# One block of linear attention and gated FFN on one core: accumulators of the last tiles moved into PSUM ahead of their passes, k weights counted by halves, and a new order of all work

## The chip, the cores and the metric

The kernel runs on one core of a Trainium2 chip. The metric is the device time of one execution in microseconds. A core has five engines that run on their own and wait for each other by semaphores: TensorE (PE, with its weight loads as PEld), VectorE (DVE), ScalarE (ACT), GpSimd (POOL) and SyncE (SP), which issues all DMAs here.

## What is computed

A residual block over 2048 tokens of width 512, everything in float32:

```python
xn = layernorm(x)                               # (2048, 512)
# A: linear attention, 32 heads of 16
q, k, v = split(xn @ wqkv)
pq, pk = phi(q), phi(k)                         # phi(t) = (t+1 if t>0 else exp(t)) + 1e-6
kv, z = pk^T v, sum(pk)                         # per head
s = ((pq @ kv) / (pq @ z + 1e-6)) @ wo
# B: gated FFN, inner width 1792
g = silu((gelu(xn @ w_gate) * (xn @ w_up)) @ w_down)
out = x + s * g
```

## The kernel before

**Precision and products.** Each float32 operand is split into a high part (a cast to fp32r on ACT, `split`'s `copy`) and a low part (source minus high part, on DVE or POOL, `split`'s `tt`). A product is three passes: high by high, and the two mixed ones (`three`). Products of 2 by 2 blocks are formed with seven instead of eight block products (`PRODUCTS`): sums of the products are built up in PSUM banks X, Y, Z (attention) and FX, FY, FZ (FFN). Bank X or FX takes several products one after the other; between two of them ACT copies the sum so far out (`saved`, `esaved`: tiles e1, u2, u3, fe1, fu2, fu3), and the next product is added onto the bank.

**Stages.** First x is loaded tile by tile (128 tokens), normalised (`ln`: statistics st, mv, ve on DVE, rstd on POOL, xn on DVE), transposed on TensorE into PSUM (pt) and split (Xh, Xl). The first four tiles, two pairs, take k and q by plain products: 12 matmuls a tile for k (`plain`, tiles k00 to k11), then 12 for q. Their weights are the k columns of `wqkv`, loaded in four requests of 256 KB: the two halves of wk1 and of wk2, which `kq_split` splits into kq. Then the other pairs go by block products, and gps gathers pk^T xn. After that the FFN of one half of the tokens runs (`ffn(1, ...)`), with the rest of the attention in between (pkv, pm, sps), and at the end the FFN of the other half (`ffn(0, finish0)`). An FFN goes over 28 quarter weights q (`quad`), with down products into accumulators `acc` by groups of units (`down`, groups [0], [1, 2], [3, 4], [5, 6]); the first group copies its bank into acc on ACT, the later ones add theirs on DVE. Behind the last group `finish0` takes silu of acc, multiplies it by s (fs, read back from DRAM), adds x (fx) and stores. The last tile (j = 7) is done in two column halves (`halves`).

**Order.** No engine's order is written out by hand. Every operation is recorded in `Plan` with an engine, a cost, its predecessors and a due time (`late`); `forward` lays them out one after the other, on each engine that one first that is ready and due earliest, and TensorE may take an operation up to `AHEAD` = 6 us out of the stated turn. It keeps one shared port for POOL and those DVE operations that don't touch PSUM, and it gives DMAs a landing time from `RATES`. Then `altered` changes due times at random, from a seed: it picks a place where TensorE waits within a stretch of turns, and shifts due times around it. The seeds that are applied are listed in `KEPT`, by stretch. So whatever changes a cost, a dependency or a seed can move any instruction on any engine. How the planner scores a seed is this:

```python
for lo, hi, draws in KEPT:
    for n in draws:
        best = self.altered(n, lo, hi, pe, *best)
```

The dependencies that matter for the change: `kq_split` used `raw[:, i]`, a view that stands for both halves of the weight, so a half was planned as if it needed both loads. In `down`, the last group ended with

```python
do("DVE", dve(D // m), lambda o, i: nc.vector.tensor_add(o, o, i), a, ps, name="acc")
```

and `finish0` then called `silu`, which works on acc in place.

Of the kernel before, what the change touches and what calls it, by code (L numbers as in the profile page):

```python
# [16 lines left out]
EPS_LN = 1e-5  # L17
EPS = 1e-6
KEPT = [
    (-1, 12, [3200031, 3200084, 3200113, 3200368]),  # L20
    (605, 9999, [3200013, 3200102, 3200161, 3200247]),
]

TABLES = {"exp": "exp", "gelu": "gelu", "silu": "silu"}
LOAD = 1.28

RATES = 215.0, 380.0

HELD = 1.9

# [55 lines left out]
class Plan:  # L86
# [71 lines left out]
    def altered(self, n, lo, hi, pe, _, done, late):  # L158
        draw = random.Random(n)
        for o in self.ops:  # L160
            o.late = late[o]
        waits = [w for w in self.waits(done) if lo <= w[0] < hi]
        if not waits:
            return _, done, late
        w = draw.choices(waits, [w[1] for w in waits])[0]
        if draw.random() < 0.5:
            for o in self.chain(done, w[2]):
                if draw.random() < 0.7:
                    o.late -= draw.uniform(0.0, 4.0)
        else:  # L170
            at, back = w[2].late, draw.uniform(1.0, 12.0)
            share, far = draw.choice((0.05, 0.2, 0.5)), draw.uniform(0.2, 4.0)
            for o in self.ops:
                if at - back < o.late < at + 2.0 and draw.random() < share:
                    o.late += draw.uniform(-far, far)
        new = self.forward(pe)
        return max(t for t, _ in new), new, {o: o.late for o in self.ops}
# [83 lines left out]
    def forward(self, pe):  # L261
        for o in self.ops:
            o.left, o.ready, o.end, o.lat, o.behind = len(o.pre), 0.0, None, o.lat0, []
        cands = {e: [] for e in self.HOP}
        free = dict.fromkeys(self.HOP, 0.0)
        port = dma = 0.0
        for o in self.ops:
            if not o.left:
                cands[o.eng].append(o)
        done, first, table, last = [], 0, "exp", {}  # L270
        while any(cands.values()):
            best = None
            while first < len(pe) and pe[first].end is not None:
                first += 1
            for e, c in cands.items():
                if e == "PE":
                    c = [o for o in c if o.turn <= pe[first].turn + self.AHEAD]
                if not c:
                    continue
                ready = {}  # L280
                for o in c:
                    t = o.ready
                    for g in o.banks:
                        p = last.get(g)
# [12 lines left out]
                if best is None or (t, asked) < best[:2]:  # L297
                    best = t, asked, o
            t, asked, o = best
            cands[o.eng].remove(o)  # L300
            if o.table and o.table != table:
                t, table = t + LOAD, o.table

            took = o.cost - (min(self.CUT[o.eng], t - asked) if o.port else 0.0)

            if o.eng == "PE" and t > free["PE"] + 0.02:
                took += 0.1
            free[o.eng] = o.end = t + took
            for g in o.banks:
                if g in last and last[g].eng != o.eng:  # L310
                    o.behind.append(last[g])
                last[g] = o
            if o.port:
                port = o.end
            if o.eng == "SP":

                dma = max(dma, o.end) + o.kb * (1.4 if o.kb == 896 else 1.0) / (RATES[0] if o.end < 3.0 else RATES[1])
                o.lat = max(dma - o.end, o.kb / self.RATE) + (0.9 if o.end < 8.0 else HELD)
            done.append((o.end, o))
            for q in o.suc:  # L320
                q.ready = max(q.ready, o.end + self.gap(o, q))
                q.left -= 1
                if not q.left:
                    cands[q.eng].append(q)
        assert len(done) == len(self.ops)
        return done
# [15 lines left out]
def kernel(  # L342
# [96 lines left out]
    def split(hi, lo, src, n, name="", eng="DVE"):  # L439
        copy("ACT", hi, src, n, name + "h")  # L440
        tt(eng, "sub", lo, src, hi, n, name + "l")
# [85 lines left out]
    def kq_split(slot, raw, k, n=1, eng="DVE"):  # L527
        r = 4 * ORDER.index(slot)
        if n == 2 and r // 7 == (r + 3) // 7:
            h = KQ[r // 7].part(KQR[slot, 0], (slice(None), slice(r % 7, r % 7 + 2)))  # L530
            lo = KQ[r // 7].part(KQR[slot, 1], (slice(None), slice(r % 7 + 2, r % 7 + 4)))
            split(h, lo, raw, n * D, f"kq{slot}", eng)
        else:
            for i in range(k, k + n):
                split(kq(slot, 0, i), kq(slot, 1, i), raw[:, i], D, f"kq{slot}", eng)

    tokens = [(8 * (n // 4) + n % 4, 8 * (n // 4) + 4 + n % 4) for n in range(NP)]

# [227 lines left out]
    for n in range(NP):  # L766
        if n == 0:
            ln(tokens[n][1])
        else:
            ln(*tokens[n])  # L770
        for i in range(2):
            load_next()
            transp(n, i)
            split_x(n, i)
            if n < CL:
                if i:
                    b = tile_in("up", 19 + n, [P, 2, 2, P], F32R, f"b12_{n}", 2)
                    b12[n] = [b.part(b.res[lo:lo + 1], (slice(None), lo)) for lo in range(2)]
                    split(*b12[n], pts[n, 1][:, 0:2], 2 * P, "b12")
                if 2 * n + i == 3:  # L780
                    gacc(first_g)
                split_xn(tokens[n][i])
                k_out(plain(n, i, False), tokens[n][i])
        if n >= CL:
            forms(n)
            if n < 2 * CL:
                forms(n - CL)
                spill_x(n - CL)
            if n < 4:
                spill_x(n)  # L790
            rest(n, first_products(n))
            for t in tokens[n]:
                gacc(t)
        if n == CL - 1:
            for t in seq[1:2 * CL]:
                gacc(t)
            for m in range(CL):
                for i in range(2):
                    q_out(plain(m, i, True), tokens[m][i])
# [162 lines left out]
    def down(p, units_, is_first, is_last, finish):  # L962
        for j in range(8):
            key = (11, 21) if j < 4 else (12, 22)
            sl = slice((j % 4) * P, (j % 4 + 1) * P)
            m = halves(p, units_, j)
            if is_first:
                acc[p, j] = tile_in("up", FACC[j], [P, D], F32, f"acc{p}_{j}", 2 if halves(p, groups[-1], j) > 1 else 1)
            for c in range(m):
                ps = bank(ring("down", [5, 6, 7]), f"d{p}_{units_[0]}_{j}{c}", (P, D // m))  # L970
                cs = slice(c * D // m, (c + 1) * D // m)
                total = Sum(ps)
                for u in units_:
                    hh, hl = hs[p, u, key[0]], hs[p, u, key[1]]
                    dh, dl = dws[p, u]
                    total.add(("D", p, u, j, c), *three([(h[0][:, sl], h[1][:, sl]) for h in (hh, hl)],
                                                       [(dh[:, i, cs], dl[:, i, cs]) for i in range(2)]),
                              name="down", cost=PASS if m == 1 else SHORT)
                a = columns(acc[p, j], c, m)
                if is_first:  # L980
                    copy("ACT", a, ps, D, "acc")
                else:
                    do("DVE", dve(D // m), lambda o, i: nc.vector.tensor_add(o, o, i), a, ps, name="acc")  # L983
            if is_last:
                finish(p, j)

    groups = [[0], [1, 2], [3, 4], [5, 6]]

    def silu(p, j, n=1):
        for i in range(n):  # L990
# [164 lines left out]
    def finish0(p, j):  # L1155
# [3 lines left out]
        dma(sr, s_d(j, slice(j * P, (j + 1) * P)), 256)  # L1159
        dma(xr, ext(x[j * P:(j + 1) * P, :]), 256)  # L1160
        w = D // n
        silu(p, j, n)
        for i in range(n):
            so = columns(sr, i, n)
            do("DVE", dve(w), lambda o, a: nc.vector.tensor_mul(o, o, a), so, columns(acc[p, j], i, n))
# [36 lines left out]
```

## Time and profile before

| | us |
|---|---|
| median of 3 runs | 625.42 (625.35 to 626.65) |
| the profiled execution | 625.18 |
| its span | 623.2 |
| PE busy | 615.2 (99%) |
| DVE, ACT, POOL busy | 408.5, 319.1, 233.0 |
| granted clock of TensorE | 0.997 |

The profile is of one execution; times in it count from the start of its span. In the chain of work that ended last, each line is a start, a duration and what ran. In the timeline, a line is a start, a duration, the engine, the line of the kernel, the operation with output and inputs, and in brackets how long the engine had been idle and what ended that. In the waits, the columns are the total, the number of times and the longest.

### The profile page before, as it was taken

The page shows a single profiled execution, that of the slowest core. Times are in us where ns is not written, and L with a number is a line of the kernel's source. Part 1 is how long each engine was busy: PE and PEld are TensorE (multiplying, and loading weights), DVE is VectorE, ACT ScalarE, POOL GpSimd, SP SyncE. Part 2 cuts the span into 40 slices and gives each one's busy share as a digit, 9 for nine tenths or more (in the row PEclk, how much of TensorE's full clock was granted, in tenths as well). Part 3 has the DMA queues.
Part 4 walks back from the last instruction along what each step waited for, and adds up shares of the span by engine and source line. Part 5 has one row for each costly group of instructions (what it writes and reads, how often), then busy time and mean ns, then how long its engine had stood idle before and what let it go on. Part 6 is the DMA issues. An engine that isn't in the chain of part 4 may idle for free.

```text
span 623.2 us, 7828 instructions
## 1 busy us (share of the span) xinstructions
PE 615.2 (99%) x2782; PEld 506.1 (81%) x2782; DVE 408.5 (66%) x648; ACT 319.1 (51%) x571; POOL 233.0 (37%) x239
## 2 busy tenths in 40 slices
PE   8999999999999999999999999999999999999996
PEld 6887888888888888888888788888888888888885
DVE  6999998787626643762448799657366427732466
ACT  6777777887556523650345332276656316612431
POOL 4447754366624520460046334044334404300110
PEclk9999999999999999999999999999999999999998
DMA  7249822135221211220169566841221212001163
GB/s 246 74 150 311 262 73 69 68 103 167 68 67 35 64 39 35 67 68 0 44 186 387 181 210 209 306 134 37 65 60 43 68 34 68 1 1 34 35 198 140
DMA packets 52440, 68.68 MB, mean 110 GB/s; under 512 B 2864, under 2 KB 31792, under 8 KB 52400
## 3 DMA queue, kind: packets, MB, share of 16 engines
q1 hardware_dynamic: 52400, 68.17, 34.0%
q8 instruction: 22, 0.36, 0.3%
q14 instruction: 18, 0.15, 0.1%
HBM read 49.28 MB, written 18.87 MB: 109 GB/s over the span
## 4 chain that ended last, share of the span: by engine, by line
PE 98%; DVE 0%; DMA 0%; ACT 0%; issue 0%; POOL 0%; DVEq 0%
PE FX L460 25%; PE d L460 24%; PE FZ L460 12%; PE sps L460 7%; PE gps L460 7%; PE FY L460 6%; PE X L460 5%; PE Z L460 3%; PE k L460 2%; PE q L460 2%; PE Y L460 1%; PE pt L624 1%; PE ptq L1115 1%; PE pkv L1075 1%; PE pm L1087 1%; DMA x<-in_A_x 0%
## 5 line engine op out<-in xcount | busy, mean ns | idle before, releaser
L460 PE MATMUL FX<-Xh,w 128*128 128x512 f32 x448 | 134.4, 391 | 0.0
L937 POOL TENSOR_TENSOR h<-h,g 128x512 f32<-128x512 f32 x42 | 59.5, 1416 | 179.1 <-DVE h L437 179.1
L460 PEld LDWEIGHTS FX<-Xh,w 128*128 128x128 f32 x448 | 83.5, 188 | 18.8 <-ACT fu L431 1.7
L437 POOL TENSOR_TENSOR tmp<-raw 128x256 f32<-128x256 f32 x56 | 45.0, 822 | 93.0 <-DVE w L437 77.9
L460 PE MATMUL d<-dwh,hh 128*128 128x512 f32 (+1 forms) x228 | 69.7, 388 | 0.0
L460 PE MATMUL d<-dwh,hl 128*128 128x512 f32 (+1 forms) x228 | 69.2, 385 | 0.0
L460 PE MATMUL FX<-Xl,w 128*128 128x512 f32 x224 | 69.1, 390 | 0.0
L460 PE MATMUL FZ<-Xh,w 128*128 128x512 f32 x224 | 69.0, 389 | 0.0
L460 PE MATMUL d<-dwl,hh 128*128 128x512 f32 (+1 forms) x228 | 68.9, 385 | 0.0
L983 DVE TENSOR_TENSOR acc<-acc,d 128x512 f32<-128x512 f32 (+1 forms) x49 | 33.0, 673 | 48.6 <-PE d L460 48.5
L431 ACT CAST hh<-h 128x512 fp32r<-128x512 f32 x56 | 34.6, 620 | 56.6 <-PE d L460 27.9
L431 ACT COPY fu<-FX 128x512 f32<-128x512 f32 x56 | 32.7, 584 | 42.3 <-PE FX L460 42.2
L460 PEld LDWEIGHTS d<-dwl,hh 128*128 128x128 f32 x228 | 42.6, 188 | 8.7
L460 PEld LDWEIGHTS d<-dwh,hl 128*128 128x128 f32 x228 | 42.5, 188 | 8.6
L460 PEld LDWEIGHTS d<-dwh,hh 128*128 128x128 f32 x228 | 42.3, 188 | 8.8 <-issue 0.5
L460 PEld LDWEIGHTS FX<-Xl,w 128*128 128x128 f32 x224 | 42.0, 188 | 8.9
L460 PEld LDWEIGHTS FZ<-Xh,w 128*128 128x128 f32 x224 | 42.1, 188 | 8.7
L437 DVE TENSOR_TENSOR w<-raw,w 128x512 fp32r<-128x512 f32 (+1 forms) x56 | 44.9, 807 | 1.7 <-ACT w L431 1.6
L437 DVE TENSOR_TENSOR hl<-h,hh 128x512 fp32r<-128x512 f32 x56 | 39.0, 700 | 9.6 <-ACT hh L431 9.6
L437 DVE TENSOR_TENSOR w<-tmp,w 128x512 fp32r<-128x512 f32 x56 | 38.4, 693 | 6.8 <-ACT w L431 6.5
L431 ACT CAST dwh<-draw 128x1024 fp32r<-128x1024 f32 x14 | 14.7, 1049 | 47.3 <-PE d L460 45.1
L437 DVE TENSOR_TENSOR g<-fu,FZ 128x512 f32<-128x512 f32 x28 | 19.1, 683 | 30.0 <-PE FZ L460 27.0
(160 smaller groups left out, 1206.5 us busy)
## 6 DMA issues: line engine op xcount, KB each, us to landing
raw<-in_B_w_gate SPq DMA_DIRECT2D x14, 512.0 KB, 3.8
raw<-in_B_w_up SPq DMA_DIRECT2D x14, 512.0 KB, 3.8
draw<-in_B_w_down SPq DMA_DIRECT2D x14, 512.0 KB, 3.4
x<-in_A_x SPq DMA_DIRECT2D x16, 256.0 KB, 4.3
q_d<-qp SPq DMA_DIRECT2D x16, 256.0 KB, 2.0
q<-q_d SPq DMA_DIRECT2D x16, 256.0 KB, 3.6
xh_d<-Xh SPq DMA_DIRECT2D x4, 896.0 KB, 5.5
xl_d<-Xl SPq DMA_DIRECT2D x4, 896.0 KB, 7.3
```

The source lines that it names most:

```text
L431: do("ACT", act(n), lambda o, i: nc.scalar.copy(o, i), dst, src, name=name)
L437: do(eng, c, lambda o, p, q: getattr(e, f"tensor_{op}")(o, p, q), dst, a, b, name=name)
L460: nc.tensor.matmul(o, a, b, start=not self.on and self.made == 1, stop=self.made == self.passes, skip_group_check=self.on)
L624: nc.tensor.transpose(o[:, k, :], a[:, k * P:(k + 1) * P], b)
L937: do("POOL", pool(NC), lambda o, i: nc.gpsimd.tensor_mul(o, o, i), h, g, name="h")
L983: do("DVE", dve(D // m), lambda o, i: nc.vector.tensor_add(o, o, i), a, ps, name="acc")
L1075: nc.tensor.matmul(o[:, g, :], a[:, c, g * P:(g + 1) * P], b[:, c, g * P:(g + 1) * P], start=(c == 0), stop=(c == KT - 1))
L1087: do("PE", 0.9, lambda o, a, b, g=g: nc.tensor.matmul(o, a[:, g, :], b[:, g, :], start=True, stop=True), pm, kv4, wo_sb, key=("m", g))
L1115: nc.tensor.transpose(o[:, k, :], a[:, k * P:(k + 1) * P], b)
```

## The change

Five things are changed. In `down`, for the tiles from `LATE` = 6 on of the last group of the last FFN half, ACT copies the accumulator into the PSUM bank ahead of the passes, the passes are added onto it, and silu is taken from PSUM into acc, where before DVE added the bank to acc and silu ran on acc; `finish0` leaves silu out for these tiles. In `kq_split`, each half of a k weight depends on its own load alone. The planner's DMA rate for the first 3 us goes from 215 to 260, and its latency there from 0.9 to 1.1. `altered` may also pick a place where TensorE does not wait, and may shift one to three operations instead of a share of them. And `KEPT` holds other seeds, in 17 stretches over the whole kernel instead of two at its ends. The condition `2 * n + i == 2 * CL - 1` is the same as before, since CL is 2.

```diff
 KEPT = [
-    (-1, 12, [3200031, 3200084, 3200113, 3200368]),
-    (605, 9999, [3200013, 3200102, 3200161, 3200247]),
+    (-1, 12, [
+        3, 6, 9, 16, 21, 23, 24, 36, 43, 59, 80, 100, 139, 165, 212, 370, 472
+    ]),
+    (12, 25, [176]),
+    (25, 40, [3, 204, 205, 209, 226]),
...
+    (500, 560, [7]),
+    (560, 605, [5]),
 ]
...
-RATES = 215.0, 380.0
+RATES = 260.0, 380.0
...
         waits = [w for w in self.waits(done) if lo <= w[0] < hi]
+        if not waits or draw.random() < 0.3:
+            waits += [(o.turn, 0.1, o) for o in pe if lo <= o.turn < hi]
...
-            share, far = draw.choice((0.05, 0.2, 0.5)), draw.uniform(0.2, 4.0)
-            for o in self.ops:
-                if at - back < o.late < at + 2.0 and draw.random() < share:
+            share, far = draw.choice((1, 2, 3, 0.05, 0.2, 0.5)), draw.uniform(0.2, 4.0)
+            near = [o for o in self.ops if at - back < o.late < at + 2.0]
+            for o in draw.sample(near, min(len(near), share)) if share >= 1 else near:
+                if share >= 1 or draw.random() < share:
                     o.late += draw.uniform(-far, far)
...
-                o.lat = max(dma - o.end, o.kb / self.RATE) + (0.9 if o.end < 8.0 else HELD)
+                o.lat = max(dma - o.end, o.kb / self.RATE) + (1.1 if o.end < 8.0 else HELD)
...
             for i in range(k, k + n):
-                split(kq(slot, 0, i), kq(slot, 1, i), raw[:, i], D, f"kq{slot}", eng)
+                split(kq(slot, 0, i), kq(slot, 1, i), half(raw, i), D, f"kq{slot}", eng)
...
-                total = Sum(ps)
+                a = columns(acc[p, j], c, m)
+
+                kept = p == 0 and is_last and j >= LATE
+                if kept:
+                    copy("ACT", ps, a, D // m, "kept")
+                total = Sum(ps, kept)
...
-                a = columns(acc[p, j], c, m)
                 if is_first:
                     copy("ACT", a, ps, D, "acc")
+                elif kept:
+                    do("ACT", act(D // m), lambda o, i: nc.scalar.activation(o, i, AF.Silu), a, ps, name="silu")
                 else:
                     do("DVE", dve(D // m), lambda o, i: nc.vector.tensor_add(o, o, i), a, ps, name="acc")
...
+    LATE = 6
...
-        silu(p, j, n)
+        if j < LATE:
+            silu(p, j, n)
```

What the new order does to the first requests: SP now issues x of tile 0, the second half of wk1, x of tile 4, the first half of wk1, and then the halves of wk2; before, it issued both x tiles and then the four halves in turn. On ACT the casts of three of the four halves now stand ahead of the cast of Xh of tile 0; before, one of four stood behind the first Xh and the others later. On POOL the low part of the second half of wk1 now stands between rstd of tile 0 and rstd of tile 4. On DVE the statistics of x of tile 4 (st, mv) now stand ahead of xn of tile 0.

More of the change, by code (lines that the diff above doesn't have):

```diff
@@ L19 @@
 KEPT = [
-    (-1, 12, [3200031, 3200084, 3200113, 3200368]),
-    (605, 9999, [3200013, 3200102, 3200161, 3200247]),
+    (-1, 12, [
[3 more added lines that the diff above has]
+    (25, 40, [3, 204, 205, 209, 226]),
+    (40, 55, [6, 9, 10, 17, 40, 145, 206]),
+    (55, 70, [
+        2, 3, 4, 13, 22, 24, 31, 106, 319, 320, 325, 330, 333, 335, 357, 358, 415
+    ]),
+    (70, 85, [
+        7, 20, 38, 52, 65, 67, 125, 144, 147, 178, 180, 181, 184, 195, 201, 232, 360, 367, 392, 400,
+        402, 430, 686, 702
+    ]),
+    (85, 100, [252, 262]),
+    (100, 115, [4, 5, 11, 13, 19, 27]),
+    (115, 135, [114, 123, 128, 302, 450]),
+    (135, 200, [
+        3, 4, 9, 11, 20, 21, 24, 30, 37, 44, 46, 51, 55, 63, 64
+    ]),
+    (200, 270, [5, 12, 32, 40, 54, 84]),
+    (270, 340, [5, 129, 133, 135, 136, 152, 153, 168, 178]),
+    (365, 385, [3, 7, 18, 34, 38]),
+    (400, 420, [3, 4, 5, 13, 15, 267]),
+    (420, 500, [5, 7, 10, 16]),
+    (500, 560, [7]),
+    (560, 605, [5]),
 ]
@@ L779 @@
                     split(*b12[n], pts[n, 1][:, 0:2], 2 * P, "b12")
[L780 removed]
+                if 2 * n + i == 2 * CL - 1:
                     gacc(first_g)
```

## The prediction

> **What bounds the kernel now.** I read the page's shares first, then the chain of work that ended last, then who waited for whom.
>
> ```profile
> span 623.2 us, 7828 instructions
> PE 615.2 (99%) x2782; PEld 506.1 (81%) x2782; DVE 408.5 (66%) x648; ACT 319.1 (51%) x571; POOL 233.0 (37%) x239
> PE 98%; DVE 0%; DMA 0%; ACT 0%; issue 0%; POOL 0%; DVEq 0%
> 219.40 21.76 PE d L460 x96
> PEld FX L460 <- ACT fu L431: 1.7, 7, 0.3
> PEld X L460 <- ACT e L431: 0.4, 2, 0.2
> PEld X L460 <- DVE qp L689: 0.3, 1, 0.3
> PEld X L460 <- DVE Xl L437: 0.3, 1, 0.3
> PEld X L460 <- ACT u L431: 0.2, 1, 0.2
> ACT hh L431 <- POOL h L937: 18.0, 19, 2.3
> ```
>
> The matmuls are the chain. 96 of them in a row take 21.76 us, so a matmul 512 wide costs 0.2267 us when nothing holds it, and the count of matmuls is the same after the change: the time can move only in the start before TensorE is dense, in the few places in the middle where it is held, and in the tail behind the last matmul. In the middle the weight loads waited 2.9 us in all, at twelve places (the five PEld rows). That is the whole stock that a better order can take away there.
>
> **The start.** The chain and the groups, to the first q product:
>
> ```profile
> 0.80 2.77 DMA x<-in_A_x
> 5.37 0.56 DVE xn L576
> 5.97 0.67 PE pt L624 x4
> 6.67 0.37 ACT Xh L431
> 7.61 0.50 PE k L460
> 7.59 0.69 DVE L437 TENSOR_TENSOR kq<-wk,kq 128x512 fp32r<-128x512 f32 x1 [0.17 <-ACT kq L431]
> 14.94 0.44 PE pt L624 x4
> 20.93 2.72 PE q L460 x12
> 1.72 1.85 SPq L427 DMA_DIRECT2D wk<-in_A_wqkv  x4
> DMA to landing us min/median/max: 3.2/3.9/4.4
> L431 ACT CAST kq<-wk 128x512 fp32r<-128x512 f32 x4 | 2.4, 626 | 0.0
> ```
>
> From the first k matmul at 7.61 to the first q at 20.93 there are 13.32 us. The work in them is 48 k matmuls (10.88) and three transposes of 0.45 (1.35), so 1.09 us is idle. The halves of the k weights are the four requests from 1.72 on: the first lands 3.2 us after its issue (4.92), the last, issued at about 3.1, 4.4 us after (7.5), so one lands about every 0.87 us. In the changed order one half of wk1 goes out second, in place of x4, and lands about 0.87 earlier than 4.92, at some 4.1 to 4.25; ACT casts it at once (4.9). Then POOL subtracts it, and that has a price on VectorE:
>
> ```profile
> 4.78 0.56 POOL L572 TENSOR_TENSOR rstd<-ve,neg_half 128x1 f32<-128x1 f32 x1 [1.96 <-DVE ve L570]
> L700 POOL TENSOR_TENSOR zacc<-zacc,kp 128x512 f32<-128x512 f32 x1 | 1.3, 1302 | 2.1 <-DVE kp L689 2.1
> 61.35 0.97 POOL L437 TENSOR_TENSOR T<-xt,T 128x256 f32<-128x256 f32 x1
> 61.80 0.80 DVE L576 TENSOR_SCALAR xn<-x,mv,rstd 128x512 f32<-128x512 f32 x1
> L576 DVE TENSOR_SCALAR xn<-x,mv,rstd x16: 524/545/803, 5.4 to 98.0; 128x512 f32<-128x512 f32 x16
> ```
>
> An xn that met a POOL operation took 803 ns instead of 545 and ended 0.28 after it (62.60 against 62.32). In the changed order POOL's subtraction of that half stands right behind rstd of tile 0: 5.37 to 6.67 by the 1302 ns row. VectorE has now put the statistics of x4 ahead of xn of tile 0, so xn meets that POOL operation and ends at 6.67 + 0.28 = 6.95 instead of 5.93. Transposes (0.04 + 0.67) 7.66, cast of Xh (0.03 + 0.37) 8.06, first k matmul 8.10: 0.49 late. The Trainium skill (SBUF — State Buffer, its section on the shared port pair) says that the pair is an exclusive lock, held for the whole instruction, and that the loser blocks fully; by that, with the full 545 ns behind POOL's end, everything would come another 0.27 later. The row above shows a loser that ends sooner, and I go by the row.
>
> In return the halves are cast before TensorE asks. The first four k matmuls run to about 9.1, when tile 4's transposes can start too (xn4 stands behind ve, some 0.2, and two subtractions of 0.69, and takes 0.55: 6.95 + 2.13 = 9.08), and the next thing that can hold is POOL's subtraction of the last half: landed 7.5, cast behind Xh and xnh to 9.37, POOL 9.41 to 10.71, against TensorE there at 10.70. I take 0.46 us idle in place of 1.09. Start: +0.49 - 0.63 = **-0.1**, with -0.6 (xn isn't held) and +0.6 (the last two POOL steps are each late by half of their 1.3) as ends.
>
> **The tail.**
>
> ```profile
> 617.62 0.42 DVE L983 TENSOR_TENSOR acc<-acc,d 128x256 f32<-128x256 f32 x1
> 618.07 0.42 ACT L991 ACTIVATE acc<-acc 128x256 f32<-128x256 f32 x1 [1.02 <-DVE acc L983]
> 618.55 0.42 DVE L1165 TENSOR_TENSOR fs<-fs,acc 128x256 f32<-128x256 f32 x1
> 618.89 0.75 DVE L437 TENSOR_TENSOR fs<-fs,fx 128x256 f32<-128x256 f32 x2
> 620.07 0.33 SPq L427 DMA_DIRECT2D out_y<-fs  x1
> ```
>
> Behind the last matmul (through at about 617.6) stand the addition into the accumulator, silu, the product, the addition of x and the store. With the accumulator in PSUM ahead of the passes, silu starts where the addition started. So 617.62 + 0.42, product 618.10 to 618.52, addition from 618.44 (0.34 behind the product, as now) to 618.86. The other half's addition no longer stands ahead of it, since that half is through 1.44 us (12 matmuls of 0.12) earlier. Store at 618.89 instead of 620.07: **-1.2**; if the 0.43 between 619.64 and 620.07 is the queue's own and stays, -0.75. The added work is three copies on ACT (two of 256, one of 512 columns). I bound one copy by the 0.37 and 0.63 us of the ACT rows here. They are hidden: the bank of tile 6 was last read 24 matmuls earlier (5.4 us), that of the last half 12 wide and 12 narrow ones (4.2 us) earlier, and that span needs an addition, a silu and a copy, at most 2.1 us. If that cover went, the last half would start up to 0.6 later. The order shows the three copies ahead of their passes, so that the change does not do this is no case.
>
> **The middle.** Here the new order decides, and the row to know is what a copy out of a bank costs when TensorE comes back to the bank soon:
>
> ```profile
> 592.19 0.62 PE L460 MATMUL FX<-Xh,w 128*128 128x512 f32 x2
> 592.90 0.59 ACT L431 COPY fu<-FX 128x512 f32<-128x512 f32 x1 [2.13 <-PE FX L460]
> 593.54 0.30 PEld L460 LDWEIGHTS FX<-Xh,w 128*128 128x128 f32 x2 [0.25 <-ACT fu L431]
> 593.55 0.72 PE L460 MATMUL FX<-Xh,w 128*128 128x512 f32 x2
> 594.11 0.62 PE L460 MATMUL FX<-Xl,w 128*128 128x512 f32 x2
> ```
>
> The second FX matmul starts at 592.42, and five issue steps later (592.42 + 5 x 0.2267 = 593.55) TensorE adds to the bank again. ACT's copy ran at once and ended at 593.49, and still the weight load waited 0.25 and the next pair came at 594.11 instead of 594.00: **0.11 lost**. The way from last matmul to next is thus 1.24 us; six matmuls (1.36) cover it, five (1.13) don't. Counted in the order of instructions before, four places behind the start stand at five (X3, X4, FX13, FX27), and 34 copies at seven. Counted in the changed order, 25 places stand at five steps or the same in transposes: 19 in the banks X and FX, five ahead of sps, and one in the accumulators of the first down group. At 0.11 each that is 2.7 us, against 0.4 today. The other eight waits of today's twelve cost by the five PEld rows 2.9 less twelve times the 0.14 that a wait of 0.25 hides (1.7), so 1.2 with the four, 0.8 without. The new order loosens many of these to nine and eleven; I keep half, 0.4. Middle: 2.7 + 0.4 - 1.2 = **+1.9**. Low end: 0.07 a place and none of the others, 1.75 - 1.2 = +0.5; high end: 0.15 a place and all others, 3.75 + 0.8 - 1.2 = +3.3.
>
> That a load waits here at all is not what a page suggests: the Trainium skill (TensorE: Matmul & The Clock Gate, Step-by-step: what each phase is for) says that TensorE pulls weight loads ahead of matmuls in flight. The 0.25 row shows that a load that carries the wait isn't pulled ahead of it; the rival that it would make is the first below.
>
> **Sum.** -0.1 - 1.2 + 1.9 = +0.6 on the profiled execution's 625.18 us (span 623.2 and 2.0 around it). That execution lies 0.24 under the median of 625.42, so I add +0.6 to the median: **626.0 us**. About 0.2% (1.25 us) is what a measurement of this kernel can tell from no change, so that is no change, on its slow side.
>
> **The rivals.** *Places at five cost nothing* (faster). The load is taken early, or the copies come sooner. Then the middle is 0 - 1.2 at best, the sum -0.1 - 1.2 - 1.2 = -2.5: 622.9, and 624 with half of it. For it: the matmul of 593.55 is shown as issued on time. Against it: the pair behind it is 0.11 late. Chance 0.15.
>
> *ACT comes late to the tight places* (slower). At six of the 19 the cast just ahead of the copy on ACT waits for a product from POOL (hh behind h). The last row of the first view has such waits: 18.0 us over 19, 0.95 on average. At seven matmuls between there was 0.35 to spare for that (1.59 - 1.24), at five there is none. From the point where POOL's product ends later than the last matmul's end, all of it is TensorE's; at 0.4 each six give 2.4, so 628.4. For it: the order was laid by a planner whose hops and costs are not the chip's (it lets five matmuls stand where 1.24 us are needed). Against it: casts stand ahead of copies today too, and ACT is busy only 51% of the span. Chance 0.27.
>
> The forecast has 0.58; its own range is 624.6 to 627.6.
>
> **How the numbers follow.** Slower by over 0.2% is above 626.67: nearly all of the second rival (0.25) and about a fifth of the forecast's cases (0.13), 0.38. Faster is below 624.17: 0.14 of the first rival and 0.02 of the rest, 0.16. Within: 0.46. The range of 8 in 10 reaches from 624.2, into the first rival, to 628.2, into the second.
>
> **What would show it.** First k matmul at about 8.1 and an xn of tile 0 that lasts over 0.8 us beside POOL; first q at 20.8; weight loads of FX waiting for fu at some 15 to 20 places instead of 7, each about 0.25; the last store 1.3 us behind the last matmul. It is wrong if FX waits of the weight loads stay at seven, or if the first k comes at 7.6 and q before 20.3.

## The result

The changed kernel takes **629.34 us** (median of 7 runs, 628.24 to 631.12) against **625.98 us** (7 runs, 625.35 to 626.66): ratio 1.0056, 95% interval 1.0045 to 1.0068. It is slower by 3.4 us; 626.0 with a range up to 628.2 was forecast. The runs of the changed kernel also spread over 2.9 us, those of the kernel before over 1.3.

The page of the profiled execution after (628.89 us, span 626.9), engine shares and the chain:

```profile
span 626.9 us, 7829 instructions
PE 618.7 (99%) x2782; PEld 505.5 (81%) x2782; DVE 409.0 (65%) x645; ACT 320.9 (51%) x574; POOL 233.9 (37%) x239
PE 94%; DMA 2%; DVE 1%; ACT 1%; issue 0%; SPq 0%; ACTq 0%
```

TensorE still carries the chain, but its share is 94% instead of 98%, with DMA, VectorE and ScalarE in place of the rest: there are stretches where TensorE waits for them. Where the 3.7 us between the two spans come in is read from the first row of each stage on TensorE's timeline. First before (first q, first X, first FX, last d):

```profile
20.77 0.39 PE L460 MATMUL q<-a,Xh 128*128 128x512 f32 x1
40.78 0.39 PE L460 MATMUL X<-kq,Xh 128*128 128x512 f32 x1
133.27 0.39 PE L460 MATMUL FX<-Xh,w 128*128 128x512 f32 x1
617.18 0.40 PE L460 MATMUL d<-dwh,hl 128*128 128x256 f32 x2
```

then after:

```profile
21.88 0.39 PE L487 MATMUL q<-a,Xh 128*128 128x512 f32 x1
41.89 0.39 PE L487 MATMUL X<-kq,Xh 128*128 128x512 f32 x1
136.11 0.39 PE L487 MATMUL FX<-Xh,w 128*128 128x512 f32 x1
621.96 0.40 PE L487 MATMUL d<-dwh,hl 128*128 128x256 f32 x2
```

| stretch | before | after | difference | forecast |
|---|---|---|---|---|
| start, to the first q | 20.77 | 21.88 | +1.11 | -0.1 |
| first q to first X | 20.01 | 20.01 | 0.00 | in the middle |
| X stage, first X to first FX | 92.49 | 94.22 | +1.73 | in the middle |
| first FX to last d | 483.91 | 485.85 | +1.94 | in the middle |
| behind the last d, to the end of the span | 6.02 | 4.94 | -1.08 | -1.2 |

The forecast's middle, +1.9 in all, was nearly all made of places in FX, sps and the down products. In its sum that part came as forecast. The start and the X stage did not.

**Behind FX.** The weight loads that waited, from the waits after (total, times, longest):

```profile
PEld FX L487 <- ACT fu L458: 3.6, 15, 0.2
PEld X L487 <- DVE qp L716: 1.5, 2, 1.2
PEld sps L487 <- ACT pqTh L458: 1.1, 5, 0.2
PE X L487 <- DVE qp L716: 0.8, 1, 0.8
PEld X L487 <- ACT e L458: 0.6, 3, 0.2
PEld pt L651 <- ACT xt L458: 0.5, 1, 0.5
PEld gps L487 <- DVE pkl L725: 0.6, 2, 0.4
```

Fifteen waits for fu instead of seven and five ahead of sps are the forecast places at five matmuls. Of the others, the rows with xt and pkl were not there before, and qp stood there with a single wait of 0.3 us. No step of the prediction has them growing.

**The X stage.** TensorE waits at 57.51 for qp. On VectorE's timeline qp stands behind the statistics of an x tile whose transfer landed at 54.94, and behind a subtraction that lasted 1.05 us:

```profile
54.97 0.69 DVE L594 BATCH_NORM_STATS2 st<-x 128x6 f32<-128x512 f32 x1 [0.71 <-DMA x<-in_A_x]
55.69 0.18 DVE L595 BATCH_NORM_AGGREGATE mv<-st 128x2 f32<-128x6 f32 x1
55.79 1.05 DVE L464 TENSOR_TENSOR Xl<-T,Xh 128x512 fp32r<-128x512 f32 x1
56.77 0.68 DVE L716 SCALAR_TENSOR_TENSOR qp<-X,qr 128x512 f32<-128x512 f32 x1
```

**The start.** TensorE's timeline, and then the windows of 1 us (busy time of the engines, and third from the right the granted clock):

```profile
6.60 0.66 PE L651 MATMUL pt<-ident,xn 128*128 128x128 f32 x4 [1.07 <-DVE ve L597]
7.85 1.49 PE L487 MATMUL k<-kq,Xh 128*128 128x512 f32 x4 [0.59 <-ACT Xh L458]
9.13 1.06 PE L651 MATMUL pt<-ident,xn 128*128 128x128 f32 x4
10.41 1.05 PE L487 MATMUL k<-kq,Xh 128*128 128x512 f32 x2
12.97 0.62 PE L487 MATMUL k<-kq,Xh 128*128 128x512 f32 x2
```

```profile
8.00:9.00 1.00, 1.00 (x4) 0.70 (x5) 1.00 (x4) 1.00 (x4) 0.00 (x0) 0.78 1.05 391
9.00:10.00 1.00, 1.00 (x6) 0.87 (x5) 1.00 (x4) 1.00 (x3) 0.82 (x1) 0.50 1.05 402
10.00:11.00 1.00, 1.00 (x4) 0.81 (x4) 0.93 (x5) 0.89 (x4) 0.46 (x1) 0.50 1.06 406
11.00:12.00 1.00, 1.00 (x4) 0.81 (x3) 0.79 (x4) 0.91 (x2) 0.70 (x1) 0.51 1.05 401
```

The clock was granted at 0.50 from 8.6 to 12.0 (the trace's own record of the granted clock has this stretch from 8.57, for 3.41 us), and two k products took 1.05 us at 10.41 but 0.62 at 12.97. The four windows add up to 0.44 + 1.00 + 1.00 + 0.98 = 3.42 us at half speed. The Trainium skill (TensorE: Matmul & The Clock Gate, What's actually happening) has a clock gate that grants half speed by TensorE's activity in free-running windows of about 3.4 us; the 3.42 agrees. It asks for a whole idle window to close the gate; in the 3.4 us ahead of 8.6 TensorE was busy for about 1.7 (the warm-up to 5.5, transposes 0.66, k products from 7.85), so a partly idle window was enough. The busy share alone is not the rule either: in the run with two more warm-up products below, full speed was granted from 4.36, TensorE was busy for about 1.6 of the next 3.4 us (warm-up to 5.6, transposes from 7.42), and it kept full speed.

**The tail** went as forecast, silu straight from the bank:

```profile
622.45 0.38 ACT L1014 ACTIVATE acc<-d 128x256 f32<-128x256 f32 x1 [1.05 <-PE d L487]
622.87 0.43 DVE L1200 TENSOR_TENSOR fs<-fs,acc 128x256 f32<-128x256 f32 x1 [0.44 <-ACT acc L1014]
623.33 0.43 DVE L464 TENSOR_TENSOR fs<-fs,fx 128x256 f32<-128x256 f32 x1
```

### The profile page after: what moved, and what is told of

It is laid out like the page before. It is cut to its first block, busy times and chain, and to the rows that moved or that the text cites. A ratio compares the mean times of both kernels' runs of the same rounds, so it can differ in the third digit from the quotient of the medians.

```text
span 626.9 us, 7829 instructions
## 1 busy us (share of the span) xinstructions
PE 618.7 (99%) x2782; PEld 505.5 (81%) x2782; DVE 409.0 (65%) x645; ACT 320.9 (51%) x574; POOL 233.9 (37%) x239
## 4 chain that ended last, share of the span: by engine, by line
PE 94%; DMA 2%; DVE 1%; ACT 1%; issue 0%; SPq 0%; ACTq 0%
PE FX L487 25%; PE d L487 24%; PE FZ L487 12%; PE sps L487 7%; PE FY L487 6%; PE gps L487 6%; PE X L487 4%; PE Z L487 2%; PE k L487 2%; PE q L487 1%; PE ptq L1149 1%; DMA x<-in_A_x 1%; PE pt L651 1%; PE Y L487 1%; DMA wk<-in_A_wqkv 1%; PE pm L1121 1%
## 5 line engine op out<-in xcount | busy, mean ns | idle before, releaser
L487 PE MATMUL FX<-Xh,w 128*128 128x512 f32 x448 | 130.7, 392 | 0.0
L487 PE MATMUL d<-dwh,hl 128*128 128x512 f32 (+1 forms) x228 | 67.9, 386 | 0.0
L1016 DVE TENSOR_TENSOR acc<-acc,d 128x512 f32<-128x512 f32 x46 | 31.4, 684 | 49.5 <-PE d L487 49.5
L464 DVE TENSOR_TENSOR hl<-h,hh 128x512 fp32r<-128x512 f32 x56 | 41.6, 745 | 15.7 <-ACT hh L458 15.5
L464 DVE TENSOR_TENSOR w<-raw,w 128x512 fp32r<-128x512 f32 (+1 forms) x56 | 42.8, 770 | 3.3 <-ACT w L458 3.0
L464 DVE TENSOR_TENSOR w<-tmp,w 128x512 fp32r<-128x512 f32 x56 | 39.7, 723 | 7.8 <-ACT w L458 7.6
L727 POOL TENSOR_TENSOR zacc<-zacc,kp 128x512 f32<-128x512 f32 x16 | 24.2, 1510 | 35.0 <-DVE kp L716 31.0
```

Source lines behind the costliest of these rows:

```text
L464: do(eng, c, lambda o, p, q: getattr(e, f"tensor_{op}")(o, p, q), dst, a, b, name=name)
L487: nc.tensor.matmul(o, a, b, start=not self.on and self.made == 1, stop=self.made == self.passes, skip_group_check=self.on)
L727: do("POOL", pool(D), lambda o, i: nc.gpsimd.tensor_add(o, o, i), zacc, p0, name="zacc")
```

## The experiments

Most of the kernels have their order of work given as a list, in place of the planner's, with the changed code otherwise:

```diff
-    for o in plan.order([part for key in pe_keys for part in subs.get(key, [key])]):
-        o.fn()
+    for n in WORK:
+        plan.ops[n].fn()
```

A list can hold one kernel's order up to a point and the other's from there on, or one order with one instruction moved. Each group of runs, on a chip of its own, has its own runs of the kernel before beside it; their medians were 625.87 (the tail alone, before's front, 23 places loosened, qp first), 626.01 (before's order up to FX, the two warm-ups, xn first), 626.09 (20 places and four places loosened, x tile 4 second, the late transfer), 625.69 (POOL's sums, both edits, the cut at 80, the last version) and 626.02 (the cuts at 50 and 62). So the same kernel's median differs by up to 0.4 us between groups, and differences across groups carry that much doubt.

### Taking the sum apart by stretches

**The tail alone**: before's order up to the last passes, then the changed tail.

> Before's order of all work up to the last passes of the last two tiles, then the changed tail (three copies ahead of the passes, silu straight from PSUM). If the tail is worth what the trace of after shows (end of span minus last matmul 1.08 us shorter), 624.9 us against 626.0 for before. If the tail's gain belongs to the new order and not to the accumulators in PSUM, 626.0. In the profile: last store about 1.2 us sooner behind the last matmul than before, TensorE's start and middle as before (first q product at 20.8, X to FX as before).

Measured 624.41 (623.91 to 625.56; ratio to before 0.9975, 0.9965 to 0.9985): -1.46. The end of the span came 4.66 us behind the start of the last d, against 6.02 before, and the first q at 21.14 with the k products as in before's order (13.15 from the first k to the first q). So the gain belongs to the changed tail and not to the order of the work ahead of it. The changed tail also has its own order of the last passes and of VectorE's work behind them; what that gives and what the accumulators in PSUM give is not separated.

**Before's front**: before's order up to the first q.

> Before's order up to the first q product, after's order from there on, tail as changed. Theory (the start costs 1.1 us by itself): 628.2 us against 629.3 for after, first q product at 20.8. Second theory (the late x request at 48 us and the wait for qp at 57 us come from the late start too): the wait of 0.8 to 1.2 us at 57 us goes as well, 627.0 to 627.4. Rival (what is lost in the start is absorbed by later waits on transfers): 629.3.

Measured 628.35 (627.70 to 629.22; ratio 1.0039): -1.0 against the changed kernel, as its profile says (first q at 20.86 instead of 21.88); the wait for qp stayed (0.8 us), so the X stage's loss does not come from the start.

**Before's order up to FX**, so that start and X stage are before's.

> Before's order from the start through the whole of the X stage (to the first FX product), after's order from there on, tail as changed. Theory (the profiles' sum: start +1.1 us, q to FX +1.7, FX to the last matmul +1.9, tail -1.1): the start and the X stage come back to before, so 626.5 us against 629.3 for after, first q at 20.8 to 21.1 and first FX at 133.3 to 133.7. Rival (the X stage was late only because the start was, and the rest was late with it): 628.3, as with before's front alone.

Measured 626.46 (626.01 to 627.63; ratio 1.0008, 0.9999 to 1.0016), as the sum of the profiles said; first q at 20.64, first FX at 133.14. So by medians: start 629.34 - 628.35 = 1.0, X stage 628.35 - 626.46 = 1.9, FX and later 626.46 - 624.41 = 2.05, tail -1.46. The sum is +3.5, of 3.4 to be explained.

### The places at five matmuls

In the changed order, the matmul pair that comes back to a bank after four others is put one place later, or another pair is put ahead of it:

```diff
 TensorE, behind the copy fu2_4
-FX (bank just copied), FX part of unit 5
+FX part of unit 5, FX (bank just copied)
```

> After, with 23 of the places at five matmuls between a bank's last matmul and its next loosened: the part that comes back to the bank is put one part later, or another part ahead of it, nothing else in the order changes. Theory (each place costs 0.11 us on TensorE): 2.5 us less, 626.8 against 629.3, and the weight loads of FX that wait for fu fall from 15 to 2 or 3. Rival (places at five cost nothing, the time went elsewhere): 629.3. Rival (half of them are late by more than the step, behind POOL's product on ScalarE): 2.5 to 4 us less.

Measured 627.28 (625.93 to 629.43; ratio 1.0027): -2.06 for 23 places, 0.09 each by the medians. The starts of the two kernels differ from execution to execution, and between the two profiles the stretches behind the first q became 1.5 us shorter (X to FX 94.06 instead of 94.22, from FX on 1.38), which is 0.07 a place. Of the rows with fu, pqTh and e one is left:

```profile
PEld FX L487 <- ACT fu L458: 0.2, 1, 0.2
```

The same from FX on, behind before's order:

> Before's order to the first FX, after's order from there (the kernel of 626.46), with 20 of the places at five matmuls from FX on loosened. Theory (what is left against before with the changed tail, 626.46 - 624.41 = 2.05, is these places at about 0.1 each): 624.3 to 624.8. Rival (only the 1.5 us that the loosened places gave between the profiles, and some of the rest is other waits of the new order): 625.0 to 625.5.

Measured 624.85 (624.35 to 626.03): -1.61 for 20 places, 0.08 each (1.43 between the profiles from FX on, 0.07 each), and 0.44 from the 624.41 that before's order reaches there. It lies between the theory's and the rival's ranges: most of the stretch's 2.05 us are these places, and a few tenths are not.

> Before's order with the changed tail (the kernel of 624.41), and the four places at five matmuls that before's order has behind the start (two in the bank X, two in FX) loosened. Theory: 4 x 0.07 to 0.11, so 623.9 to 624.1, which is at the limit of what can be measured. Rival (the places moved cost elsewhere): 624.4 or more.

Measured 624.78 (624.03 to 626.02), no gain over 624.41: the four places of before's order are too few to see. Its profile had first q at 21.72, so the start below blurs it too, and X to FX 92.73 where the tail alone had 92.52, so the two places moved in X gave nothing.

### The start: which wait, and the half speed

**Two more warm-up products** in the changed kernel, **two fewer** in the kernel before:

```diff
-    def warm(o, w, n=WARM):
+    def warm(o, w, n=WARM + 2):
```

> After, with 12 warm-up products instead of 10 on TensorE, order and planned costs unchanged, so that TensorE is busy to about 6.6 us, when the first transposes can run, instead of 5.7. Theory (TensorE runs the first k products at half speed because it stood idle for about 1.1 us ahead of the transposes): the k products come every 0.23 us from the first on, start 0.9 to 1.7 us shorter, 627.6 to 628.4 against 629.3, and the runs' spread (2.9 us) is smaller. Rival (the half speed has nothing to do with the idle time, or the time of the start hangs on when the transfers land alone): 629.3 or, where the transposes now wait for the warm-up, up to 629.6.

> Before, with 8 warm-up products instead of 10 on TensorE, all else unchanged, so that TensorE is idle for about 1.1 us ahead of the first transposes instead of 0.25, as in after. Theory (that idle time brings TensorE's half speed back): the first k products come every 0.43 us or more for 2 to 4 us, start 0.9 to 1.7 us longer, 626.8 to 627.6 against 625.9 for before. Rival (idle time there costs nothing, since the transposes wait for xn either way): 625.9.

More: 628.41 (627.65 to 630.95; ratio 1.0043, 1.0030 to 1.0057), -0.9, with an interval that overlaps the changed kernel's. Fewer: 627.56 (626.50 to 628.42; ratio 1.0023, 1.0013 to 1.0032), +1.55 over the 626.01 beside it. TensorE's timeline with two fewer:

```profile
5.97 1.12 PE L624 MATMUL pt<-ident,xn 128*128 128x128 f32 x4 [1.06 <-DVE xn L576]
10.36 0.63 PE L460 MATMUL k<-kq,Xh 128*128 128x512 f32 x1
10.79 0.63 PE L460 MATMUL k<-kq,b 128*128 128x512 f32 x1
```

and with two more:

```profile
7.42 0.66 PE L651 MATMUL pt<-ident,xn 128*128 128x128 f32 x4 [1.83 <-DVE ve L597]
8.54 1.21 PE L487 MATMUL k<-kq,Xh 128*128 128x512 f32 x4 [0.46 <-ACT Xh L458]
```

With the shorter warm-up the transposes still started at 5.97, but the k products then came every 0.43 us, and the first q at 23.27 instead of 20.77: what changed is TensorE's pace, and by the medians it cost 1.55 us. That pace is the shown cause of a late start. It lasted longer than the 2 to 4 us of the expectation, and it did not come back after the idle time: the trace's first record of full speed stands at 13.89 us, so that TensorE had not left half speed by then. (Slow transposes are no sign by themselves: in four profiles of before's front with the full warm-up they took 1.11 or 1.12 as well, but full speed came at 6.9 to 7.0, ahead of the k products, and k to q took 13.15.) With the longer warm-up full speed stood from 4.36 on, the four k products took 1.21 instead of 1.49, and the first q came at 21.20 although the transposes started 0.8 later than in the changed kernel's profile. From the first k to the first q that is 12.66 us, where the changed kernel took 14.03 in the same order (one profile of each). What failed of the expectation is the spread, which stayed at 3.3 us, and that the idle time there was 1.83 us and yet no half speed came: it isn't the length of one idle time that decides.

**xn of tile 0 ahead of the statistics of tile 4**, on VectorE:

```diff
 VectorE
-st, mv of tile 4
 xn of tile 0
+st, mv of tile 4
```

> After, with one edit of VectorE's order: xn of tile 0 ahead of the statistics of tile 4, as in before. Theory (in after, xn of tile 0 stands behind the landing of x4, which is now the third transfer, 4.9 to 5.6 us): first transposes at about 5.9 instead of 6.6 to 7.0, whatever x4 does, TensorE's idle time there shrinks, first q at 20.9 to 21.4 instead of 21.8 to 23.4, 628.2 to 628.8 against 629.3, with less spread. xn then meets POOL's subtraction of the k half (5.0 to 6.3 us): if the shared port blocks it whole, xn ends at 6.8 and nothing is gained, 629.3 (rival).

Measured 630.38 (628.63 to 631.27; ratio 1.0068, 1.0055 to 1.0081), no gain: the rival. (The median is 1.0 higher, but the intervals overlap.) VectorE's and POOL's timelines:

```profile
5.25 1.48 DVE L603 TENSOR_SCALAR xn<-x,mv,rstd 128x512 f32<-128x512 f32 x1 [0.68 <-POOL rstd L599]
5.18 1.26 POOL L464 TENSOR_TENSOR kq<-wk,kq 128x512 fp32r<-128x512 f32 x1
```

xn lasted 1.48 us instead of 0.55 and ended 0.29 behind POOL's subtraction (5.18 + 1.26 = 6.44). First transposes 6.78, k products at half pace until the trace's first record of full speed at 13.60, first q 23.22.

**x tile 4 second**, on SP:

```diff
 SP
 x tile 0
-wk1 half 1, x tile 4
+x tile 4, wk1 half 1
```

> After, with one edit of SP's order: the transfer of x tile 4 second, as in before, and the half of wk third. Theory (the start is late because xn of tile 0 stands behind the statistics of tile 4, whose transfer lands at 4.9 to 6.0 us): x4 lands by 4.6, the first transposes start at about 6.0, TensorE's idle time ahead of them is short, first q at 20.9 to 21.4, 628.2 to 628.6 against 629.3. Rival (the half of wk now lands just so late that POOL's subtraction starts ahead of xn and holds it to its end, as in the run with xn first: 1.48 us instead of 0.55): first transposes at 6.8 or later, 629.3 to 630.4.

Measured 629.48 (627.70 to 630.05), no gain. The transposes started at 6.07 as expected, and xn was not held. But the casts of the halves still stood ahead of Xh on ScalarE, the first k product came at 8.01, and the clock was at 0.50 again (3.42 us in all), first q at 22.08.

Put together, from the profiles: in the changed kernel's order and its variants the first k product started between 7.85 and 8.58 and the time from there to the first q was 12.66 to 14.87; in before's order 7.49 to 8.11, and 13.15 in ten profiles and 14.07 in three (one chip). The clock records tell two cases apart. In five profiles full speed was granted and taken back for 3.41 us, at 7.69 to 8.91 (the changed kernel, x tile 4 second, and three of before's front); in four it was first granted late, at 10.49 (the places loosened), 13.60, 13.70 (qp first) and 13.89. In the other eleven it came at 4.36 to 7.02 and stayed. So the half speed can come with either order. Of the six profiles of the changed order only the one with the longer warm-up was free of it; of the thirteen of before's front with 10 or 11 warm-up products ten were.

### The X stage

**qp first** on VectorE, ahead of the late tile's statistics:

```diff
 VectorE, 55 to 57 us
-st of the late tile, mv, Xl, qp
+qp, st of the late tile, mv, Xl
```

> After, with one edit of VectorE's order: the product qp, for which TensorE waits at 57.5 us, stands ahead of the statistics of the x tile whose transfer lands at 54.9 us, instead of behind them and a subtraction. Theory (qp stands in the queue behind a late transfer): the wait of TensorE at 57 us goes, 0.8 to 1.2 us, so 628.1 to 628.5 against 629.3, and the spread of the runs (628.2 to 631.1) gets smaller, since a transfer's landing no longer decides. Rival (the statistics pushed back make the next tile late instead): 629.3, with a new wait of transposes for xn behind 62 us.

Measured 630.59 (629.82 to 632.26). The wait for qp at 57 us went, but X to FX took 94.73 instead of 94.22. VectorE now stood idle ahead of qp for ScalarE's qr (first line below), and TensorE had other waits in its place (the rest):

```profile
57.34 0.69 DVE L716 SCALAR_TENSOR_TENSOR qp<-X,qr 128x512 f32<-128x512 f32 x1 [1.57 <-ACT qr L714]
PEld gps L487 <- DVE pkl L725: 1.0, 2, 0.5
PEld pt L651 <- PE X L487: 0.8, 1, 0.8
PEld gps L487 <- DVE xnl L464: 0.6, 1, 0.6
PE pt L651 <- DVE xn L603: 0.4, 1, 0.4
```

The start of this profile was late besides (first q at 23.40); the edit has no part in that.

**The late transfer asked for earlier**, on before's front (from here on the comparison is 628.35, X to FX 94.12):

```diff
 VectorE, 45 to 48 us
-kq subtraction, ve, Xl, c, xn
+ve, kq subtraction, xn, Xl, c
 SP
-spill of Xl, x tile
+x tile, spill of Xl
```

> Before's front, after's order from the first q on (the kernel of 628.35), with the x tile that lands late at 54 us asked for about 1.2 us earlier: VectorE's ve and xn, which free its buffer, stand 0.6 to 1.2 us earlier in VectorE's order, and SP issues it ahead of the spill of Xl. Theory (the transfer's landing starts VectorE's late stretch, and TensorE's wait for qp at 56 us with it): the wait of 0.94 us goes and the small ones behind it shrink, 626.9 to 627.5. Rival (VectorE's queue itself is too long in 50 to 70 us, the transfer is only what it happens to wait for; the edit that put qp first moved the wait and gained nothing): 628.3 to 628.9, with waits of the same sum at other places.

Measured 628.42. The statistics no longer waited for the transfer and what TensorE lost there fell from 0.94 to 0.12 us, yet X to FX was 94.06. The rival's time came, and the wait moved; that VectorE's queue is too long is its reading, which this run does not show.

**POOL's four sums of the gate weights later**, alone and with the earlier transfer:

```diff
 POOL
-tmp, tmp, T3, T4, tmp, tmp, zacc
+T3, T4, tmp, tmp, zacc
```

> Before's front, after's order from the first q on (the kernel of 628.35), with one edit of POOL's order: the four sums of the gate weights (tmp), which stand ahead of the third and fourth T product of one tile and ahead of the next tile's, go behind them, as before has them. Theory (POOL's sums make T late and lengthen VectorE's operations in 60 to 70 us): X to FX 93.0 to 93.5 instead of 94.1, 627.2 to 627.7. Rival (the stage hangs on VectorE's idle time at the late transfer): X to FX 94.1, 628.3.

> The same kernel with both edits: POOL's four sums later and the x tile asked for 1.2 us earlier. Theory (VectorE's queue is the bound in this stretch, and each edit alone only moves its debt on): X to FX 92.5 to 92.9, 626.7 to 627.1. Rival (neither is the cause; it is the order of VectorE's own operations): X to FX 94.0 or more, 628.3.

Measured 628.66 and 628.16; X to FX 94.54 and 93.95. Both theories fell. POOL's edit left the wait for qp where it was (0.78 us in its profile); the two edits of VectorE's order took it away. None of the three, at three engines, gave more than 0.2 us in X to FX.

**Where the order is cut**: before's order up to 80, 50 and 62 us of the plan, after's from there.

> Before's order up to 80 us, after's order from there on, tail as changed. Theory (all that the X stage loses lies between 50 and 75 us): X to FX 92.5, and 626.5 as with before's order up to FX. Rival (part of it lies behind 80 us): X to FX 92.8 to 93.5, 626.8 to 627.5.

> Before's order up to 50 us of the plan, after's order from there on, tail as changed. Theory A (after's order makes its debt in the first 9 us of the X stage, where VectorE's subtractions for kq stand ahead of the statistics that free the x buffer, and the waits of 57 to 72 us are its late payment): X to FX 92.5 to 92.9, 626.5 to 626.9. Theory B (the debt is made by the order between 50 and 75 us itself): X to FX 93.6 to 94.2, 627.7 to 628.3.

> Before's order up to 62 us of the plan, after's order from there on, tail as changed. By theory A of the cut at 50: 92.5 to 92.9, 626.5 to 626.9. By theory B something between 92.6 and 93.6, 626.6 to 627.7, as the part of the debt that lies behind 62 us stays.

| before's order up to | time, us | X to FX |
|---|---|---|
| first q (20) | 628.35 | 94.12 |
| 50 | 628.69 | 94.10 |
| 62 | 627.92 | 93.65 |
| 80 | 626.74 | 92.58 |
| FX (131) | 626.46 | 92.49 |

So 1.1 of the 1.6 us are made by the order between 62 and 80 us, 0.45 between 50 and 62, and nothing at 41 to 50: theory B, though the two times (628.69 and 627.92) and the 93.65 lie a little above its ranges. VectorE's timeline at 62 to 72, with the cut at 80 (before's order there), and then with the cut at 62 (after's):

```profile
65.25 0.68 DVE L464 TENSOR_TENSOR xnl<-xn,xnh 128x512 fp32r<-128x512 f32 x1
65.85 1.23 DVE L725 SCALAR_TENSOR_TENSOR pkl<-kp,pkh 128x512 fp32r<-128x512 f32 x1
67.13 0.42 DVE L464 TENSOR_TENSOR Xl<-pt,Xh 128x256 fp32r<-128x256 f32 x1
```

```profile
65.17 0.73 DVE L716 SCALAR_TENSOR_TENSOR kp<-c,kr 128x512 f32<-128x512 f32 x1
67.07 0.42 DVE L464 TENSOR_TENSOR Xl<-pt,Xh 128x256 fp32r<-128x256 f32 x1 [1.18 <-ACT Xh L458]
67.42 0.88 DVE L464 TENSOR_TENSOR xnl<-xn,xnh 128x512 fp32r<-128x512 f32 x1
69.17 1.14 DVE L725 SCALAR_TENSOR_TENSOR pkl<-kp,pkh 128x512 fp32r<-128x512 f32 x1
```

In before's order VectorE does xnl and pkl while the transposes of the next tile run; with the cut at 62 it stands idle for 1.18 us for Xh and does pkl at 69.17, 3.3 us later, and TensorE waits for it. TensorE's waits in that stretch with the cut at 62:

```profile
PEld gps L487 <- DVE pkl L725: 0.6, 1, 0.6
PEld pt L651 <- ACT xt L458: 0.5, 1, 0.5
```

Neither row is there in that stretch with the cut at 80. ScalarE's order differs as well. Its copy xt of the transposes, for which TensorE waits, stands ahead of VectorE's Xl with the cut at 80, and behind it with the cut at 62:

```profile
63.53 0.59 ACT L458 COPY xt<-pt 128x512 f32<-128x512 f32 x1
```

```profile
65.33 0.59 ACT L458 COPY xt<-pt 128x512 f32<-128x512 f32 x1 [1.17 <-DVE Xl L464]
```

TensorE's wait for xt, 0.5 us, is there in every profile with the changed order behind 62 us and in none with before's up to 80. Whether the place of xt on ScalarE or that of pkl and xnl on VectorE is the cause was not tried: the cuts move all engines' orders at once.

### The version that the runs point to

Before's order, the changed tail, and one more warm-up product:

> Before's order with the changed tail (the kernel of 624.4) and 11 warm-up products instead of 10. Theory (half speed of TensorE comes in some executions of before's start too, and a longer warm-up keeps it away): k to q 12.7 to 13.2 us in the profile, less spread, 623.6 to 624.2. Rival (the warm-up now ends behind xn and holds the first transposes, and the half speed comes or not as before): 624.4 to 624.6.

Measured **623.77** (623.54 to 624.27; ratio to before 0.9971, 0.9959 to 0.9982), faster than both kernels. By its interval it can't be told from the tail alone (0.9975). Its spread of 0.7 us is the smallest of all runs, but k to q was 13.15 in its profile as without the extra product, so that the warm-up helped the median is not shown.

## Why the prediction was wrong

**Start, -0.1 forecast, +1.1 in the profile and +1.0 by the medians.** The first k product was put at 8.10; it came at 7.85, and at 8.35 to 8.58 in most other profiles of that order, so this step was about right. Its price held too: xn ended 0.27 us behind POOL's subtraction (0.28 was taken). But xn started only at 5.78, behind the statistics of tile 4, whose transfer is now third and landed at 4.9 to 6.0; it lasted 0.76 us. The step that failed is that 48 k products were counted at 0.2267 us each. At half clock they came every 0.43 us, and between the first k and the first q stood 1.80 us beyond the counted work (14.03 less 10.88 and 1.35), where 0.46 was forecast. With the longer warm-up and full speed the same order left 0.43 (12.66 less the same): the idle time was sized well, and the other 1.37 us are TensorE's pace, for which the prediction had no term, although the later xn and the casts ahead of Xh, which it did list, leave TensorE idle there. A smaller error is a reading: 20.93 is where the chain's row of q starts, while the first q product starts at 20.77, so that before had 0.93 us idle and not 1.09, and the forecast should have been about 0.0.

**Middle, +1.9 forecast, +3.7 measured.** The number of the places at five was about right (15 to 20 waits for fu and five ahead of sps were counted on, 15 and five came), and their price was put too high, at 0.11 against 0.07 to 0.09. From FX to the last d the sum came to +1.94, but at 0.07 to 0.09 the 20 loosened places are only 1.4 to 1.6 of that; a few tenths are waits that no term had, so that the agreement there is in part luck. The step that failed is the term "the other waits": 0.8 today, 0.4 after, taken from the instruction distances alone. It was to shrink by 0.4; instead the X stage became 1.73 us longer. There VectorE is nearly always busy (9.87 of 10 us from 60 to 70 in the profile before), and the cuts show that the order of the work between 50 and 80 us makes 1.5 of the 1.6 us between the two orders. That this is the order on VectorE and ScalarE, which the count of matmuls between two uses of a bank does not see, is read from their timelines; which operation it hangs on stays open.

**Tail, -1.2 forecast:** -1.08 in the profile, -1.46 by the run of its own. The copies were hidden as described, and the matmuls ran on beside them.

**The rivals.** Places at five cost nothing: refuted, 0.07 to 0.09 each. ScalarE late to the tight places behind POOL's h: it gave the time nearest to the result (628.4), but for a reason that did not happen: loosening 23 places gave 2.06 us, not the 2.5 + 2.4 that this rival would have let go. "Slower" had a chance of 0.38 and came, by two causes that had none, so that its coming is luck and does not speak for the working. Of the signs, the 15 waits for fu came and the first q at 20.8 did not.

## What to carry to other kernels

A sum over an order of work has to hold a term for every stretch in which a second engine is nearly as busy as the bound one, and not only for the places that can be counted. A wait named at the end of such a stretch is no price: in two runs here it was taken away, and waits of the same sum came elsewhere. And where a kernel starts with a warm-up, work that is moved ahead of the first real matmuls can cost twice: its own time, and the pace of the matmuls behind it.

## What the runs showed of the hardware

- TensorE started at half speed in all twenty profiles: warm-up matmuls came every 0.21 us, and every 0.11 where full speed was granted before they ended. Full speed was first granted at 4.27 to 7.02 us in sixteen of them and at 10.49 to 13.89 in four, although the warm-up began at 1.1 us in all of them. In five of the sixteen it was taken back for 3.41 us, within the first 9 us. Leaving out 2 of 10 warm-up products, 0.8 us of work that feeds nothing, cost 1.55 us.
- In two profiles the windows show a granted clock of 1.00 while k products came every 0.43 us. These traces hold no clock record yet at that time: the first stands at 13.89 (two fewer warm-up products) and 13.60 (xn first), and there the products change to one every 0.23 us. So a 1.00 ahead of the first record says nothing, and the distance between like matmuls is what to read.
- An operation of VectorE that ran beside one of POOL from its beginning (5.25 against 5.18) lasted 1.48 us instead of 0.55 and ended 0.29 behind POOL's. Held back whole it would have ended 0.55 behind. In the changed kernel's profile xn ended 0.27 behind, and 0.28 in the row that the prediction used.
